# Pooled attention with a squared-relu feed-forward: the front written in another order, plain copies of probabilities, relu first in a step, longer groups of idle products

## The chip, the core and the metric

The kernel runs on one core of a Trainium2 chip. It uses five engines, each with a queue of its own that is worked off in order: TensorE (PE, with its weight loads as PEld), VectorE (DVE), ScalarE (ACT), GpSimd (POOL), and SyncE (SP), which here only issues DMAs. The metric is the device time of one execution in microseconds, the median of three runs. Lower is better.

## The reference

Attention with eight heads over 8 batches of 576 tokens, in which keys and values are averaged over groups of 8 tokens (72 keys remain), and then a feed-forward layer whose activation is the square of a relu. All is float32.

```python
k_p = k.reshape(B, H, Sp, pool, D).mean(axis=3)      # 576 keys -> 72
v_p = v.reshape(B, H, Sp, pool, D).mean(axis=3)
scores = scale * np.matmul(q, k_p.transpose(0, 1, 3, 2))
scores = scores - np.max(scores, axis=-1, keepdims=True)
attn = np.exp(scores)
attn = attn / (np.sum(attn, axis=-1, keepdims=True) + 1e-09)
x = np.matmul(attn, v_p)             # then heads side by side: [4608, 512]
h = np.maximum(x @ w_in, 0.0)        # w_in [512, 2048]
out = h * h @ w_out                  # w_out [2048, 512]
```

## The kernel before

The 4608 tokens are worked in 12 chunks of 384 (`CH`). A chunk's feed-forward is 16 steps (`NFC`), one for each block of 128 hidden columns: `hidden` forms the block's products with `w_in` (tile `h`), `activate` applies relu and square on ScalarE (tile `r`), and two steps later (`LAG`) `project` multiplies by `w_out` and adds into three accumulators (tile `o`). The attention of a later chunk is spread over the steps of the chunks ahead of it by the table `work`, which holds for each step the functions to run in it. In chunk 0 the first six blocks use plain float32 products (8 records per `h`); from then on operands are split into a high part (made by ScalarE) and a low part (made by VectorE), with three products of each pair.

Ahead of step 0 stands the front, written out by hand: the attention of chunk 0, when nothing is there to hide it. Names in traces: `k`, `q`, `v`, `vv` are loads; `kp` pooled keys, each in two copies; `kps`, `qps` transposes of keys and queries on TensorE, which ScalarE copies to `kf` and `st`; `sps` the scores of one pair of heads; `tm` their maxima and `te` their exponentials (`token_scores`); `token_normalise` divides `te` by its sums on VectorE; `pps` are `te` turned by TensorE (`token_turn`) and copied to `sc` by ScalarE; `vps` pooled values (`pool_v_pair`); `av` the weighted values (`weigh_values`), copied to `x`. There are four pairs of heads. `idle` are products of the identity whose result nobody reads (`keep_busy(n)`: n products, two records each). Chunk 1 runs the same token-wise functions inside chunk 0's steps (table `EARLY`); later chunks use another form.

The weights arrive as float32 words in `raw_i` (from `w_in`) and `raw_o` (from `w_out`), 512 KB each, and pass through `magnitude` (two instructions on ScalarE) and, a step later, `to_float32` (three on VectorE per tile; two tiles as a rule), giving `wf_i` and `wf_o`; `split_weights` then makes `w_i`, `w_o`. So in chunk 0 ScalarE and VectorE prepare weights while TensorE already uses them. `split_x0` makes `xh` and `xl` from chunk 0's `x`.

Within a step the instructions are written in this order: `hidden`; the attention's products; `project`; what follows on those products; the other work of the step (`magnitude` among it); `to_float32`; `split_weights`; the DMA issues; `activate`. Each engine keeps that order. All instructions carry line 34, that of the recording helper, in the profile.

Of the kernel before, what the change touches and what calls it, by code (L numbers as in the profile page):

```python
# [37 lines left out]
def pooled_attn_relu2_ffn(  # L38
# [35 lines left out]
    SCALE = 1.0 / (D ** 0.5) / POOL  # L74
    LAG, QL = 2, 4

    IDLE = (10, 2)
    STB, SCB, LD, OB = 1, 2, 4, 3


# [5 lines left out]

    STEADY = ((-22, -18, -14, -10), (0, 1, 3, 4, 5, 6, 7, 8))
    KV0 = -35
    EARLY = ((-16, -13, -10, -7), (0, 1, 2, 3, 4))

    KV_AT = ((0, 1, 4, 5, 8, 9), (2, 3, 6, 7, 10, 11), (7, 12), (12, 13, 16, 17, 20, 21, 24, 25))
    NKT = H * SP_ // QT
# [121 lines left out]
    def pool_k(b, i):  # L214
        if i % KT == 0:
            loaded["kp", b, i // KT] = sb.tile([QT, KT, 2, D], F32, name=f"kp_{b}_{i}", tag="kp", bufs=2)
        kp, kt = loaded["kp", b, i // KT][:, i % KT], loaded.pop(("k", b, i))
        if b == 1:
            by_halves(kp[:, 0, :], kt)
            GP.tensor_tensor(kp[:, 1, :], kt[:, :D], kt[:, D:2 * D], op=ALU.add)  # L220
        else:
            DVE.tensor_reduce(kp[:, 0, :], kt.rearrange("p (o d) -> p d o", d=D), axis=AX.X, op=ALU.add)
            DVE.tensor_copy(kp[:, 1, :], kp[:, 0, :])

    def new_batch(b):
        if b not in kv:
# [171 lines left out]

    def token_banks(c, p, name, tag):
        if c:
            return [ps_a.tile([P, 512], F32, name=f"{name}_{c}_{p}_{j}", tag="a") for j in range(2)]
        if tag == "h":
            return [ps_h.tile([P, 512], F32, name=f"{name}_{c}_{p}_{j}", tag="h") for j in range(2)]
        return [ps_o.tile([P, 512], F32, name=f"{name}_{c}_{p}_{j}", tag=f"o{(2 * p + j) % NTT}") for j in range(2)]

    def token_scores(c, p):
        st = live.pop((c, p))
        ss = token_banks(c, p, "sps", "o")  # L410
        segs = segments(c)
        for t in range(NQ):
            h, b = 2 * p + t // 2, segs[t % 2 % len(segs)][0]
            for j in range(2):
                two = slice(j * D, (j + 1) * D)
                PE.matmul(ss[j][:QT, t * SP_:(t + 1) * SP_], lhsT=st[two, t * QT:(t + 1) * QT],
                          rhs=kf[b][two, h // KH, h % KH * SP_:(h % KH + 1) * SP_], start=True, stop=True)
        views = [x[:QT, :NQ * SP_].rearrange("p (t n) -> p t n", t=NQ) for x in ss]

        def then():  # L420
            m = sb.tile([QT, 4, 2, NQ], F32, name=f"tm_{c}_{p}", tag="tm", bufs=2)
            e = w_tile(F32, f"te_{c}_{p}")[:QT, :, :NQ * SP_].rearrange("p i (t n) -> p i t n", t=NQ)
            e = [e[:, i] for i in range(2)]
# [12 lines left out]

        return then
# [10 lines left out]
    def token_turn(c, p):  # L448
        e, _ = live.pop((c, p))
        pt = token_banks(c, p, "pps", "h")  # L450
        for i in range(2):
            for t in range(NQ):
                PE.transpose(pt[i][:SP_, t * QT:(t + 1) * QT], e[t // 2][:, i * 2 + t % 2], ident[:QT, :QT])

        def then():
            sc = sb.tile([SP_, 2, CH], F32, name=f"sc_{c}_{p}", tag="sc", bufs=SCB)
            order = "p (s t two) -> p two t s" if len(segments(c)) == 1 else "p (t s two) -> p two t s"
# [9 lines left out]
    def split_x0():  # L467
        xts[0] = [sb.tile([P, NPAIR, CH], F32R, name=f"{x}_0", tag=x, bufs=2) for x in ("xh", "xl")]
        for i, x in enumerate(x0):
            split(*(t[:, 2 * i:2 * i + 2] for t in xts[0]), x)  # L470

    def weigh_values(c, p):

# [7 lines left out]
        for b, o, n in segments(c):  # L481
            for i in range(2):
                PE.matmul(av[i * D:(i + 1) * D, o:o + n], lhsT=kv[b][2][:, 2 * p + i, :], rhs=sc[:, i, o:o + n],
                                 start=True, stop=True)

        def then():
            if c == 0:
# [51 lines left out]
    def project(c, fc):  # L539
# [12 lines left out]
        def store():  # L552
            for t in range(NTT):
                ob = sb.tile([P, DM], F32, name=f"ob_{c}_{t}", tag="ob", bufs=OB)
                ACT.copy(ob, accs[c][t])
                dma(out[c * CH + t * P:c * CH + (t + 1) * P, :], ob)

        return store if fc == NFC - 1 else None

# [4 lines left out]
    def at(step, f, *a):  # L564
        work.setdefault(max(step, -PRO), []).append((f, a))
# [26 lines left out]
        land(key)  # L592
    issue_loads()
    keep_busy(IDLE[0])
    for i in range(KT + 2):
        pool_k(0, i)
    transpose_k(0, 0)()
    transpose_q(0, 0)()
    transpose_q(0, 1)()
    pool_k(0, KT + 2)  # L600
    keep_busy(IDLE[1])
    after = [token_scores(0, 0), transpose_k(0, 1)]
    for f in after:
        f()
    after = [pool_v_pair(0, 0), pool_v_pair(0, 1), token_scores(0, 1)]
    for f in reversed(after):
        f()
    after = [pool_v_pair(0, 2), pool_v_pair(0, 3)]
    transpose_q(0, 2)()
    transpose_q(0, 3)()  # L610
    for f in after:
        f()
    for i in range(NKT):
        pool_k(1, i)
    new_batch(1)
    for h in range(H):
        pool_v(1, h)
    for p in range(NPAIR):
        token_normalise(0, p)
        after = [token_scores(0, p + 2)] if p + 2 < NPAIR else []  # L620
# [63 lines left out]
    for s in range(-PRO, len(steps) + LAG):  # L684
# [51 lines left out]
```

## Time and profile before

| | |
|---|---|
| median of 3 runs | 964.59 us (963.69 to 967.23) |
| the profiled execution | 964.33 us |
| its span, first to last instruction | 962.6 us |
| TensorE busy | 946.1 us, 98% |
| VectorE busy | 615.0 us, 64% |
| ScalarE busy | 451.5 us, 47% |
| GpSimd busy | 348.8 us, 36% |

Shares are means over a long steady part and a short first one. The front and the steps of chunk 0 fill about the first eighth of the span, and it is there that TensorE has gaps and a lower clock. A start in a timeline is the time at which an instruction began; where several run one after the other, the distance of two starts is what one of them costs its queue, and the duration that is shown holds a tail that overlaps with the next.

### The profile page before, as it was taken

How to read it: one execution, taken by the hardware profiler on the slowest of the kernel's cores; microseconds unless marked ns; L12 is line 12 of the kernel's file. 1: busy time of each engine (PE TensorE's matmuls, PEld its weight loads, DVE VectorE, ACT ScalarE, POOL GpSimd, SP SyncE). 2: the span in 40 equal slices, each digit the busy share in tenths (PEclk: the TensorE clock that was granted, in tenths of full speed). 3: DMA queues.
4: the chain of work that ended last, by engine and by line, in shares of the span. 5: the costliest groups of instructions: out<-in, count | busy, mean ns of one | idle time of the engine just before them, and what ended most of it. 6: DMA issues, size and time to landing. Idle time of an engine off the chain costs nothing.

```text
span 962.6 us, 13481 instructions
## 1 busy us (share of the span) xinstructions
PE 946.1 (98%) x4944; PEld 803.6 (83%) x4944; DVE 615.0 (64%) x1028; ACT 451.5 (47%) x909; POOL 348.8 (36%) x215
## 2 busy tenths in 40 slices
PE   7899999999999999999999999999999999999998
PEld 6456668888888888888888888888888888888997
DVE  7889886667865566677765656767776565453221
ACT  3789776754444344444344344434443434532322
POOL 3800144444444434344353444344443534440000
PEclk9799999999999999999999999999999999999999
DMA  9963112113112112112112112112211110100000
GB/s 256 319 237 116 61 33 78 35 50 98 52 31 77 32 34 67 48 52 82 52 44 77 30 35 79 38 30 69 82 50 39 68 32 18 58 10 9 33 1 34
DMA packets 51651, 63.65 MB, mean 66 GB/s; under 512 B 13936, under 2 KB 32192, under 8 KB 51584
## 3 DMA queue, kind: packets, MB, share of 16 engines
q1 hardware_dynamic: 51584, 62.78, 21.2%
q8 instruction: 39, 0.64, 0.3%
q14 instruction: 28, 0.23, 0.1%
HBM read 53.08 MB, written 9.68 MB: 65 GB/s over the span
## 4 chain that ended last, share of the span: by engine, by line
PE 88%; DVE 5%; DMA 4%; ACT 2%; issue 1%; SPq 0%; ACTq 0%; DVEq 0%
PE o L34 41%; PE h L34 39%; PE av L34 3%; PE sps L34 3%; DVE wf_o L34 2%; DVE wf_i L34 1%; PE qps L34 1%; DMA raw_o<-in_moe_w_out_dram 1%; DMA v<-in_v_dram 1%; DMA k<-in_k_dram 1%; ACT te L34 1%; DMA vv<-in_v_dram 1%; DMA raw_i<-in_moe_w_in_dram 1%; DVE tm L34 1%; DVE w_i L34 1%
## 5 line engine op out<-in xcount | busy, mean ns | idle before, releaser
L34 PE MATMUL h<-xh,w_i 128*128 128x384 f32 x1488 | 416.9, 341 | 0.0
L34 PE MATMUL o<-w_o,gh 128*128 128x512 f32 x1056 | 334.8, 398 | 0.0
L34 PEld LDWEIGHTS h<-xh,w_i 128*128 128x128 f32 x1488 | 272.8, 188 | 10.6 <-issue 1.4
L34 POOL PARTITION_ALL_REDUCE tot<-sc x80 | 201.4, 2564 | 210.1 <-issue 199.6
L34 PE MATMUL h<-xl,w_i 128*128 128x384 f32 x744 | 249.9, 336 | 0.0
L34 PEld LDWEIGHTS o<-w_o,gh 128*128 128x128 f32 x1056 | 192.4, 188 | 51.9 <-issue 16.5
L34 POOL PARTITION_ALL_REDUCE mx<-sc x80 | 117.8, 1519 | 287.1 <-ACT sc L34 287.1
L34 DVE TENSOR_TENSOR gl<-r,gh 128x384 fp32r<-128x384 f32 x176 | 143.5, 815 | 109.1 <-ACT gh L34 108.9
L34 PE MATMUL o<-w_o,gl 128*128 128x512 f32 x528 | 209.1, 396 | 0.0
L34 DVE TENSOR_TENSOR r<-r 128x384 f32<-128x384 f32 x160 | 105.6, 660 | 109.1 <-ACT r L34 108.8
L34 ACT CAST gh<-r 128x384 fp32r<-128x384 f32 x176 | 90.4, 514 | 150.3 <-DVE r L34 149.8
L34 PEld LDWEIGHTS h<-xl,w_i 128*128 128x128 f32 x744 | 139.7, 188 | 10.6 <-issue 2.9
L34 ACT ACTIVATE r<-h 128x384 f32<-128x384 f32 x192 | 94.2, 491 | 100.5 <-PE h L34 99.1
L34 PEld LDWEIGHTS o<-w_o,gl 128*128 128x128 f32 x528 | 99.1, 188 | 22.1
L34 DVE TENSOR_TENSOR st<-qps,st 64x384 fp32r<-64x384 f32 x80 | 60.8, 760 | 59.1 <-ACT st L34 58.3
L34 ACT CAST st<-qps 64x384 fp32r<-64x384 f32 x80 | 59.5, 744 | 56.9 <-PE qps L34 56.5
L34 ACT CAST xh<-rb 128x384 fp32r<-128x384 f32 x40 | 20.5, 513 | 94.6 <-DVE rb L34 94.6
L34 ACT ACTIVATE sc<-sc 72x384 f32<-72x384 f32 x80 | 39.7, 525 | 46.4 <-DVE sc L34 46.4
L34 DVE TENSOR_REDUCE vp<-v 72x64 f32<-72x512 f32 x48 | 51.0, 1062 | 0.0
L34 PE MATMUL av<-sc,vp 72*64 72x384 f32 (+1 forms) x256 | 45.6, 436 | 3.6 <-ACT sc L34 2.1
L34 PE MATMUL o<-wf_o,r 128*128 128x512 f32 x96 | 44.4, 598 | 0.0
L34 DVE TENSOR_REDUCE kp<-k 96x64 f32<-96x512 f32 x42 | 43.8, 1043 | 0.2 <-DMA k<-in_k_dram 0.2
(82 smaller groups left out, 702.1 us busy)
## 6 DMA issues: line engine op xcount, KB each, us to landing
k<-in_k_dram SPq DMA_DIRECT2D x48, 192.0 KB
out_dram<-ob SPq DMA_DIRECT2D x36, 256.0 KB
raw_i<-in_moe_w_in_dram SPq DMA_DIRECT2D x16, 512.0 KB
raw_o<-in_moe_w_out_dram SPq DMA_DIRECT2D x16, 512.0 KB
v<-in_v_dram SPq DMA_DIRECT2D x56, 144.0 KB
rb<-rd SPq DMA_DIRECT2D x80, 96.0 KB
q<-in_q_dram SPq DMA_DIRECT2D x30, 192.0 KB
q<-in_q_dram SPq DMA_DIRECT2D x32, 96.0 KB
```

The costliest lines, as they stand in the source:

```text
L34: return lambda *a, **k: self.tc.keep_in_program_order(f(*a, **k))
```

## The change

It has six parts.

1. The front is written in another order. Pooled keys and scores of the first two pairs come first; the pooling of values moves from one place behind the first scores into the loop over the pairs, ahead of each `token_turn`. The second copy of batch 0's pooled keys moves from VectorE to ScalarE.
2. The front's softmax takes the form that chunk 1 had already: instead of a VectorE subtraction and two ScalarE exponentials of 288 columns, two small VectorE multiplications and eight ScalarE exponentials of 72 columns with a bias.
3. `token_turn` copies probabilities to `sc` as they stand instead of into token order. The columns of chunks 0 and 1 thus stay in another order down to `out`, where the store puts the rows back: six stores of 32 to 96 rows for a chunk instead of three of 128. Chunk 1's `weigh_values` reads its columns in two strided groups.
4. In chunk 0's steps `activate` is written ahead of the step's other work instead of last.
5. Groups of idle products have six products instead of two, and there are nine of them after the first group of ten instead of five.
6. `split_x0` is done in two halves in steps 3 and 4 instead of in one in step 3, and chunk 1's first pair starts one step later.

```diff
-    IDLE = (10, 2)
+    IDLE = (10, 6)
-    EARLY = ((-16, -13, -10, -7), (0, 1, 2, 3, 4))
+    EARLY = ((-15, -13, -10, -7), (0, 1, 2, 3, 4))
...
-            DVE.tensor_copy(kp[:, 1, :], kp[:, 0, :])
+            (DVE.tensor_copy if b else ACT.copy)(kp[:, 1, :], kp[:, 0, :])
...
             for i in range(2):
                 DVE.tensor_reduce(m[:, 0, i], views[i], axis=AX.X, op=ALU.max)
-                if c:
-                    DVE.tensor_scalar(m[:, 1, i], m[:, 0, i], -SCALE, None, op0=ALU.mult)
-                else:
-                    DVE.tensor_tensor(e[i], views[i], m[:, 0, i].unsqueeze(2).to_broadcast([QT, NQ, SP_]), op=ALU.subtract)
+                DVE.tensor_scalar(m[:, 1, i], m[:, 0, i], -SCALE, None, op0=ALU.mult)
             for i in range(2):
-                if c == 0:
-                    ACT.activation(e[i], e[i], AF.Exp, scale=SCALE)
-                for t in range(NQ if c else 0):
+                for t in range(NQ):
                     ACT.activation(e[i][:, t], views[i][:, t], AF.Exp, bias=m[:, 1, i, t:t + 1], scale=SCALE)
...
-                ACT.copy(sc[:, i].rearrange(order, t=NQ // 2, two=2),
-                         pt[i][:SP_, :CH].rearrange("p (two t s) -> p two t s", t=NQ // 2, two=2))
+                ACT.copy(sc[:, i], pt[i][:SP_, :CH])
...
+                rows = rows.rearrange("(s t two) d -> two t s d" if c == 0 else "(t s two) d -> two t s d", t=2, two=2)
+                for n in range(NQ):
+                    lo, hi = max(n * QT, t * P), min((n + 1) * QT, (t + 1) * P)
+                    if lo < hi:
+                        dma(rows[n // 2, n % 2, lo - n * QT:hi - n * QT, :], ob[lo - t * P:hi - t * P, :])
...
     for p in range(NPAIR):
-        token_normalise(0, p)
-        after = [token_scores(0, p + 2)] if p + 2 < NPAIR else []
+        f = pool_v_pair(0, p)
+        if p + 2 < NPAIR:
+            g = token_scores(0, p + 2)
+            f()
+            token_normalise(0, p)
+            g()
+        else:
+            f()
+            token_normalise(0, p)
         if p:
+            keep_busy(IDLE[1])
             weigh_values(0, p - 1)()
-        keep_busy(IDLE[1])
+            keep_busy(IDLE[1])
         if p == 2:
             for key in first_keys:
                 magnitude(key)
         token_turn(0, p)()
-        for f in after:
-            f()
     to_float32(*first_keys)
+    keep_busy(IDLE[1])
     weigh_values(0, NPAIR - 1)()
...
-    at(3, split_x0)
+    for i in range(2):
+        at(3 + i, split_x0, i)
...
         for f in later:
             f()
+        if activate and s < NFC:
+            activate()
+            activate = None
         for f, a in todo:
```

Three places show how the queues change. First TensorE's queue in the second half of the front, from the idle products behind `av` of pair 1 to `av` of pair 3. Before:

```order
L34 MATMUL idle_0_444<-ident 128x128 x2
L34 MATMUL pps_2_0_452<-ident,te_2_381 72x96 x4
L34 MATMUL pps_2_1_453<-ident,te_2_381 72x96 x4
L34 MATMUL av_2_471<-sc_2_462,vp_184 64x384 x2
L34 MATMUL idle_0_475<-ident 128x128 x2
L34 MATMUL pps_3_0_478<-ident,te_3_427 72x96 x4
L34 MATMUL pps_3_1_479<-ident,te_3_427 72x96 x4
L34 MATMUL av_3_497<-sc_3_488,vp_184 64x384 x2
```

And after the change:

```order
L34 MATMUL idle_0_486<-ident 128x128 x6
L34 MATMUL pps_2_0_498<-ident,te_2_364 72x96 x4
L34 MATMUL pps_2_1_499<-ident,te_2_364 72x96 x4
L34 MATMUL vps_3_511<-vv_3_101,ones 72x128 x6
L34 MATMUL idle_0_525<-ident 128x128 x6
L34 MATMUL av_2_532<-sc_2_508,vp_179 64x384 x2
L34 MATMUL idle_0_536<-ident 128x128 x6
L34 MATMUL pps_3_0_543<-ident,te_3_415 72x96 x4
L34 MATMUL pps_3_1_544<-ident,te_3_415 72x96 x4
L34 MATMUL idle_0_562<-ident 128x128 x6
L34 MATMUL av_3_569<-sc_3_553,vp_179 64x384 x2
```

The groups of idle products are three times as long, one more stands ahead of each `av`, and the pooled values `vps` of the pair stand in the queue too.

Next ScalarE's queue in steps 2 and 3 of chunk 0 (two weight tiles' `magnitude` and the relu and square `r_2`), up to the first cast of `x` to `xh`. Before:

```order
L34 ACTIVATE wf_i_0_604<-raw_i_2_519 128x512
L34 ACTIVATE raw_i_2_519<-raw_i_2_519 128x512
L34 ACTIVATE wf_o_633<-raw_o_520 128x512
L34 ACTIVATE raw_o_520<-raw_o_520 128x512
L34 ACTIVATE r_2_655<-h_2_620 128x384
L34 ACTIVATE r_2_655<-r_2_655 128x384
L34 COPY sc_0_681<-pps_0_0_663 72x2x192
L34 COPY sc_0_681<-pps_0_1_664 72x2x192
L34 COPY st_0_553<-qps_1_673 128x384
L34 CAST xh_685<-x_0_404 128x768
L34 CAST xh_685<-x_1_405 128x768
```

And after the change:

```order
L34 ACTIVATE r_2_703<-h_2_668 128x384
L34 ACTIVATE r_2_703<-r_2_703 128x384
L34 ACTIVATE wf_i_0_655<-raw_i_2_591 128x512
L34 ACTIVATE raw_i_2_591<-raw_i_2_591 128x512
L34 ACTIVATE wf_o_708<-raw_o_592 128x512
L34 ACTIVATE raw_o_592<-raw_o_592 128x512
L34 COPY st_0_648<-qps_1_729 128x384
L34 ACTIVATE r_3_738<-h_3_724 128x384
L34 ACTIVATE r_3_738<-r_3_738 128x384
L34 CAST xh_741<-x_0_435 128x768
```

`r_2` and `r_3` now stand ahead of the magnitudes of their steps and `r_3` ahead of `xh`; of `xh` only the first half stands here.

Last VectorE's queue at the normalising of chunk 1's first pair (`tm_0`, `te_0`) and the low part `xl` of chunk 0's `x`. Before:

```order
L34 TENSOR_REDUCE tm_0_588<-te_0_589 96x4 x2
L34 TENSOR_SCALAR tm_0_588<-tm_0_588 96x8
L34 RECIPROCAL tm_0_588<-tm_0_588 96x8
L34 TENSOR_TENSOR te_0_589<-te_0_589,tm_0_588 96x288 x2
L34 TENSOR_SCALAR wf_o_516<-wf_o_516 128x512
L34 TENSOR_SCALAR wf_i_0_604<-wf_i_0_604 128x512
L34 SCALAR_TENSOR_TENSOR wf_o_516<-wf_o_516,raw_o_119 128x512
L34 SCALAR_TENSOR_TENSOR wf_i_0_604<-wf_i_0_604,raw_i_0_509 128x512
L34 SCALAR_TENSOR_TENSOR wf_o_516<-raw_o_119,wf_o_516 128x512
L34 SCALAR_TENSOR_TENSOR wf_i_0_604<-raw_i_0_509,wf_i_0_604 128x512
L34 TENSOR_TENSOR xl_686<-x_0_404,xh_685 128x768
L34 TENSOR_TENSOR xl_686<-x_1_405,xh_685 128x768
```

And after the change:

```order
L34 SCALAR_TENSOR_TENSOR wf_o_588<-raw_o_119,wf_o_588 128x512
L34 SCALAR_TENSOR_TENSOR wf_i_0_655<-raw_i_0_581,wf_i_0_655 128x512
L34 TENSOR_TENSOR xl_742<-x_0_435,xh_741 128x768
L34 TENSOR_REDUCE tm_0_689<-te_0_690 96x4 x2
L34 TENSOR_SCALAR tm_0_689<-tm_0_689 96x8
L34 RECIPROCAL tm_0_689<-tm_0_689 96x8
L34 TENSOR_TENSOR te_0_690<-te_0_690,tm_0_689 96x288 x2
```

The normalising stood ahead of the tiles `o119` and `i509` and of both `xl`; now it stands behind the same two tiles (the second is named `i581`) and behind the first `xl`.

## Rows read from the trace of the kernel before

**Rows 1.** Windows of the span: busy per engine, granted clock, DMA share.
```profile
26.00:33.00 7.00, 4.52 (x27) 2.32 (x26) 6.62 (x17) 6.00 (x12) 6.07 (x12) 0.99 0.90 254
...
33.00:43.00 10.00, 9.65 (x25) 4.85 (x24) 5.90 (x10) 5.37 (x10) 9.37 (x13) 0.50 1.03 389
...
100.00:120.00 20.00, 17.69 (x89) 11.93 (x88) 15.89 (x31) 13.69 (x31) 3.38 (x2) 1.00 0.11 37
...
160.00:960.00 800.00, 799.14 (x4179) 701.75 (x4177) 484.63 (x768) 338.59 (x670) 298.76 (x150) 1.00 0.15 47
```

**Rows 2.** TensorE's timeline in the front: start, us, what, [idle before].
```profile
8.29 0.84 PE L34 MATMUL qps<-ident,k 96*128 96x96 f32 x4
...
12.08 2.81 PE L34 MATMUL vps<-vv,ones 96*72 96x128 f32 x24 [0.49 <-DMA vv<-in_v_dram]
...
21.96 0.71 PE L34 MATMUL idle<-ident 128*128 128x128 f32 x4
...
22.29 0.39 PE L34 MATMUL idle<-ident 128*128 128x128 f32 x2
...
22.51 0.83 PE L34 MATMUL pps<-ident,te 96*72 96x96 f32 x8
...
23.27 0.90 PE L34 MATMUL sps<-kf,st 64*96 64x72 f32 x16
...
24.10 1.42 PE L34 MATMUL av<-sc,vp 72*64 72x384 f32 x4
...
39.83 4.47 PE L34 MATMUL h<-x,wf_i 128*128 128x384 f32 x8
```

**Rows 3.** TensorE's timeline in chunk 0's steps.
```profile
49.73 2.85 PE L34 MATMUL h<-x,wf_i 128*128 128x384 f32 x8 [1.17 <-ACT r L34]
...
56.20 2.85 PE L34 MATMUL h<-x,wf_i 128*128 128x384 f32 x8 [1.04 <-ACT r L34]
...
58.88 0.82 PE L34 MATMUL pps<-ident,te 96*72 96x96 f32 x8
...
59.88 2.77 PE L34 MATMUL o<-wf_o,r 128*128 128x512 f32 x6
...
102.29 0.87 PE L34 MATMUL av<-sc,vp 72*64 72x192 f32 x8 [1.56 <-ACT te L34]
```

**Rows 4.** ScalarE's timeline.
```profile
23.05 1.56 ACT L34 COPY sc<-pps 72x384 f32<-72x384 f32 x2 [1.00 <-PE pps L34]
...
40.31 0.67 ACT L34 ACTIVATE wf_o<-raw_o 128x512 f32<-128x512 f32 x1
...
45.96 0.69 ACT L34 COPY kf<-kps 128x288 f32<-128x288 f32 x2
...
51.72 1.78 ACT L34 ACTIVATE te<-sps,tm 96x72 f32<-96x72 f32 x8 [1.48 <-DVE tm L34]
...
55.62 0.53 ACT L34 ACTIVATE r<-h 128x384 f32<-128x384 f32 x1
...
60.97 1.58 ACT L34 CAST xh<-x 128x768 fp32r<-128x768 f32 x2
```

**Rows 5.** VectorE's timeline.
```profile
55.18 0.80 DVE L34 TENSOR_REDUCE tm<-te 96x4 f32<-96x288 f32 x2
...
57.19 0.42 DVE L34 TENSOR_SCALAR wf_o<-wf_o 128x512 f32<-128x512 f32 x1
...
61.85 1.83 DVE L34 TENSOR_TENSOR xl<-x,xh 128x768 fp32r<-128x768 f32 x2 [1.50 <-ACT xh L34]
...
63.59 0.42 DVE L34 TENSOR_SCALAR wf_i<-wf_i 128x512 f32<-128x512 f32 x1
...
66.67 0.70 DVE L34 TENSOR_TENSOR w_i<-wf_i,w_i 128x512 fp32r<-128x512 f32 x1
...
67.27 0.46 DVE L34 TENSOR_REDUCE tm<-sps 96x4 f32<-96x288 f32 x1
```

**Rows 6.** SyncE's issues of the stores: ns min/median/max.
```profile
L34 SPq DMA_DIRECT2D out_dram<-ob x36: 332/362/1040, 145.2 to 959.8; - x36
```

More of the change, by code (lines that the diff above doesn't have):

```diff
@@ L456, in then @@
             sc = sb.tile([SP_, 2, CH], F32, name=f"sc_{c}_{p}", tag="sc", bufs=SCB)
-            order = "p (s t two) -> p two t s" if len(segments(c)) == 1 else "p (t s two) -> p two t s"
             for i in range(2):
-                ACT.copy(sc[:, i].rearrange(order, t=NQ // 2, two=2),
-                         pt[i][:SP_, :CH].rearrange("p (two t s) -> p two t s", t=NQ // 2, two=2))
+                ACT.copy(sc[:, i], pt[i][:SP_, :CH])
             live[c, p] = (sc, None)
@@ L465, in pooled_attn_relu2_ffn, with split_x0 @@
     x0 = []
[L467 to L470, printed above, removed]
+    def split_x0(i):
+        if i == 0:
+            xts[0] = [sb.tile([P, NPAIR, CH], F32R, name=f"{x}_0", tag=x, bufs=2) for x in ("xh", "xl")]
+        split(*(t[:, 2 * i:2 * i + 2] for t in xts[0]), x0[i])
     def weigh_values(c, p):
@@ L480, in weigh_values @@
         av = ps_a.tile([P, 512], F32, name=f"av_{c}_{p}", tag="a")
-        for b, o, n in segments(c):
+        segs = segments(c)
+        for t, (b, o, n) in enumerate(segs):
             for i in range(2):
-                PE.matmul(av[i * D:(i + 1) * D, o:o + n], lhsT=kv[b][2][:, 2 * p + i, :], rhs=sc[:, i, o:o + n],
-                                 start=True, stop=True)
+                x, y = av[i * D:(i + 1) * D, :CH], sc[:, i]
+                if c == 1:
+                    x, y = (a.rearrange("p (two t s) -> p t two s", two=2, t=2)[:, t] for a in (x, y))
+                elif c:
+                    x, y = x[:, o:o + n], y[:, o:o + n]
+                PE.matmul(x, lhsT=kv[b][2][:, 2 * p + i, :], rhs=y, start=True, stop=True)
         def then():
@@ L555, in store @@
                 ACT.copy(ob, accs[c][t])
-                dma(out[c * CH + t * P:c * CH + (t + 1) * P, :], ob)
+                rows = out[c * CH:(c + 1) * CH]
+                if c > 1:
+                    dma(rows[t * P:(t + 1) * P, :], ob)
+                    continue
+                rows = rows.rearrange("(s t two) d -> two t s d" if c == 0 else "(t s two) d -> two t s d", t=2, two=2)
[3 more added lines that the diff above has]
+                        dma(rows[n // 2, n % 2, lo - n * QT:hi - n * QT, :], ob[lo - t * P:hi - t * P, :])
         return store if fc == NFC - 1 else None
@@ L594, in pooled_attn_relu2_ffn @@
     keep_busy(IDLE[0])
-    for i in range(KT + 2):
+    for i in range(KT):
         pool_k(0, i)
@@ L598, in pooled_attn_relu2_ffn @@
     transpose_q(0, 0)()
+    keep_busy(IDLE[1])
+    pool_k(0, KT)
+    f = token_scores(0, 0)
     transpose_q(0, 1)()
+    f()
+    pool_k(0, KT + 1)
+    keep_busy(IDLE[1])
+    f = token_scores(0, 1)
     pool_k(0, KT + 2)
-    keep_busy(IDLE[1])
-    after = [token_scores(0, 0), transpose_k(0, 1)]
-    for f in after:
-        f()
[L605 to L608, printed above, removed]
     transpose_q(0, 2)()
+    f()
+    transpose_k(0, 1)()
     transpose_q(0, 3)()
-    for f in after:
-        f()
     for i in range(NKT):
@@ L618, in pooled_attn_relu2_ffn @@
     for p in range(NPAIR):
-        token_normalise(0, p)
-        after = [token_scores(0, p + 2)] if p + 2 < NPAIR else []
+        f = pool_v_pair(0, p)
+        if p + 2 < NPAIR:
+            g = token_scores(0, p + 2)
+            f()
+            token_normalise(0, p)
+            g()
+        else:
+            f()
+            token_normalise(0, p)
         if p:
+            keep_busy(IDLE[1])
             weigh_values(0, p - 1)()
-        keep_busy(IDLE[1])
+            keep_busy(IDLE[1])
         if p == 2:
@@ L627, in pooled_attn_relu2_ffn @@
         token_turn(0, p)()
-        for f in after:
-            f()
     to_float32(*first_keys)
+    keep_busy(IDLE[1])
     weigh_values(0, NPAIR - 1)()
```

## Prediction

> **What bounds the kernel now.** I read the windows of the span first, to see where TensorE is not the bound. From 160 to 960 us it is busy 799.14 of 800 us at the full clock; the change touches nothing there except the order of the columns of chunk 1 and the stores of two chunks, so what it is worth is decided in the first 120 us [rows 1]. There, from 26 to 33 TensorE is busy 4.52 of 7 us; from 33 to 43 the granted clock is 0.50, the lower of the two levels (1.2 GHz); and from 100 to 120 it is busy 17.69 of 20 at the full clock, so 2.3 us are lost [rows 1]. Then I read TensorE's own timeline for the price of each kind of product and for what ended its waits [rows 2, 3], and last those of ScalarE and VectorE, which make what TensorE waits for [rows 4, 5]. The first `h` starts at 39.83 and takes 4.47 us at the low clock; a like one takes 2.85 at the full clock [rows 2, 3]. In the steps the third and fourth `h` wait 1.17 and 1.04 us for ScalarE's `r`, and an `av` waits 1.56 at 102 us [rows 3].
>
> **The front.** TensorE now has 54 idle products in groups behind the first ten instead of 10. Two idle products (four records) start at 21.96, their last two records at 22.29, and the next work at 22.51: 0.55 us for a group of two, 0.11 for each further record, so a group of six (eight records more) costs 0.55 + 0.88 = 1.43 [rows 2]. Nine of them are 12.9 us, five of the old 2.75: 10.2 us of work are added. Before, this stretch was full of waits, so most of it is hidden; what counts is whether the queue without any wait is longer than before. Its pieces are, by distances of starts or durations less their tails: `vps` four times 1.37 (12.08, two pairs in 2.81) 5.5; `pps` four times 0.76, 3.0; `sps` four times 0.83, 3.3; `av` four times some 1.37, 5.5; four more groups of transposes at about 0.35, 1.4 [rows 2]. From the first transposes, over by about 8.9 (8.29 plus half a microsecond), that is 8.9 + 12.9 + 5.5 + 3.0 + 3.3 + 5.5 + 1.4 = 40.5. I add 1.1 for two waits for ScalarE's copies that no idle group covers (the second half's pooled keys, and `kf` of that half; two such copies take 0.57 [rows 4]; 0 and 2 are the ends). The first `h` then starts at about 41.6: **+1.8**. The ends are +0.7 without the two waits and +3 with longer ones.
>
> The softmax of one pair of heads is 1.06 us of maxima (67.27, two reduces and two small multiplications), 1.65 of exponentials (51.72 less its tail) and 2.01 of normalising (from 55.18 to 57.19): 4.7 us [rows 4, 5]. One pair's share of TensorE's queue with two idle groups, `vps`, `pps`, `sps` and `av` is 7.2 us, so the new form of the softmax, and ScalarE's copies of pooled keys under the first idle products, cost nothing; without that cover a late normalising would cost up to 2.0 each. The plain copies to `sc` save ScalarE perhaps a third of the 1.56 that two took [rows 4]; TensorE's queue is the bound there, so I put that at nothing too.
>
> **The clock.** The fall at 33 follows a stretch in which TensorE was busy two thirds of the time, and the change fills that stretch with products [rows 1]. I expect the full clock up to the first `h` and behind it: 4.47 becomes 2.85, **-1.6** [rows 2, 3]. The Trainium skill (TensorE: Matmul & The Clock Gate, "What's actually happening") says that the throttled level is the default and that activity releases it; the fall behind the sparse stretch agrees, and by it the -1.6 comes. Its Part 4 there, "PE-mode transpose", says that transposes don't count as activity in the same way; no run here shows that yet, and by it the first rival below would come.
>
> **Relu first.** ScalarE gets to the last front copy some 2.0 us later than before (at 41.95; the magnitudes behind it stood at 40.31 and now follow at 42.3). Then come five pairs of magnitudes (from 40.31 to 45.96 before, 5.65) to 48.0, `kf` 0.57, `r_0` 1.0, so the third `h` still waits about as long [rows 4]. But `r_1` now stands ahead of the fourth step's magnitudes: the 1.04 of the fourth `h` goes, less what ScalarE is late, **-0.8** [rows 3]. Against it, in step 1 the copy of chunk 1's queries `st` now comes behind another pair of magnitudes, at 52.2, while TensorE is at `sps_0` at 51.7: **+0.5**.
>
> **VectorE behind `xh`.** This is the largest term. The low part `xl` needs ScalarE's `xh`, and stands now ahead of the normalising of chunk 1's first pair; before it stood behind it (rows of the order above). Before, VectorE waited 1.50 there [rows 5]. ScalarE after `r_0` (49.6): two pairs of magnitudes at 1.13, 51.9; `st` 0.4; `r_1` 1.0, 53.2; two pairs, 55.5; `te_0` 1.65, 57.1; `r_2` 1.0; two pairs, 60.4; `st` 0.4; `r_3` 1.0; so `xh`'s first half starts at 61.7 and, at half of 1.58, is there at 62.5 [rows 4]. VectorE has its maxima by 56.0 and one pair of tiles (from 63.59 to 66.67, 3.08) by 59.1, and then waits some 3.5 us: `xl` half of 1.83 to 63.4, normalising 2.01 to 65.4 [rows 5]. TensorE reaches `pps_0` at 64.1 (two `h` at 2.7 and two `o` at 2.6 behind `sps_0` [rows 3]); its first product needs only the first half of `te`: **+1.0**. What stands behind it in TensorE's queue is `sps_1` and the whole feed-forward. Before, `pps_0` at 58.88 had no wait [rows 3].
>
> The same again a step later: VectorE does a pair and a split (0.60) to 69.1, `tm_1` to 70.2, and waits 3.0 us for the second `xh` (ScalarE: `te_1` from 69.7, `r_4`, `xh` at 72.4); then `xl`, a pair and the split of the first `w_i` end at 77.7 [rows 4, 5]. TensorE stands at `h_6`, the first block that needs split weights, at 75.3 and at the product that needs the low part of them at 76.5: **+1.2**. The next normalising (2.01) ends at 80.2, when TensorE has reached `pps_1` at 78.9: **+1.3**. From there two pairs are some 2 us behind their places, and the `av` that waited 1.56 waits about **1.1 more**. Each of these four lies between 0 (ScalarE and VectorE catch up in the stretch's idle time) and about twice the value.
>
> **At nothing.** The stores: SyncE issues one in 0.36 us (median of 36), so six more are 2.2 us of a queue that has 800 us; uncovered, behind the last of a chunk, about 1 us [rows 6]. The strided reads in chunk 1's `weigh_values` are bounded by the `av` of 0.87 for eight records, four of them: between 0 and 1 us in all [rows 3]; I take 0.
>
> **The sum.** 1.8 - 1.6 - 0.8 + 0.5 + 1.0 + 1.2 + 1.3 + 1.1 = +4.5. The profiled execution took 964.33, 0.26 below the median of the runs, so 968.8.
>
> **Rivals.** (a) The clock falls in the front all the same, as it did at 33 with half-filled queues: then ten microseconds at 0.50 do the work of five, and the queue, which has no slack now, ends 5.1 later: 973.9, slower. For it: idle products and transposes are what fills the queue. Against it: from 26 to 33, with such groups in it, the clock was still 0.99 [rows 1]. It decides from about 2 us at half clock on (1 us lost). (b) VectorE's lateness is absorbed: the four terms behind `xh` and that of `st` (5.1) vanish, and 1.8 - 1.6 - 0.8 = -0.6 gives 963.7. For it: VectorE waits for ScalarE there, and each does less than it could; against it, both waits lie in a chain of `te`, `r` and `xh` that is written in that order. (c) The other sign: on top of (b) the two waits of the front do not occur (-1.1) and the freed ScalarE takes away the third `h`'s 1.17 and the 2.3 lost from 100 to 120: 963.7 - 1.1 - 1.2 - 2.3 = 959.1, faster; it decides where at least 4.6 of these 5.2 us come. Against it: the rows at 100 us wait for chunk 1's softmax, on which only its place has changed [rows 3].
>
> **Chances.** The forecast, 966.5 to 971: 0.50. (b), 962.5 to 966.5: 0.25. (c), below 962.5: 0.12. (a), above 971: 0.13. The range 961.5 to 971.5 leaves out (a) and half of (c), 0.19; the likeliest case alone is 966.5 to 971. A difference of 0.5% (4.8 us) is about what a measurement of this kernel can tell from no change: below 959.8 lies half of (c), 0.06; above 969.4 all of (a) and 0.21 of the forecast, 0.34; between them 0.60.
>
> **What the profile would show.** A granted clock of 1.00 from 9 us on, the first `h` at 41.6 and 2.85 long; no wait for `r` at the fourth `h`; VectorE waiting over 3 us for `xh` twice; waits of 1 us or more at `pps_0`, `h_6` and `pps_1`. The prediction is wrong if VectorE meets no such wait, if the front's queue still has many waits (then it is longer than 40.5), or if the clock falls.

## The result and the profile after

The changed kernel took 966.94 us (median of 20 runs, 965.63 to 969.64) beside 964.39 for the kernel before (20 runs on the same chip); the ratio is 1.0023, 95% interval 1.0012 to 1.0033: slower by 2.2 us (1.2 to 3.2). The two medians alone lie 2.6 us apart, the means of the same runs 2.2. The forecast was 968.8 with a range of 961.5 to 971.5, and 0.60 on a change of less than 0.5%; that came in. The profiled execution took 966.62 with a span of 964.9, 2.3 above the span of before.

The windows of the changed kernel (columns as in [rows 1]):

```profile
9.00:26.00 17.00, 16.51 (x175) 14.44 (x175) 14.37 (x36) 11.26 (x47) 9.35 (x21) 1.00 1.06 294
26.00:33.00 7.00, 7.00 (x63) 6.28 (x62) 4.51 (x11) 4.03 (x10) 6.53 (x12) 1.00 0.90 259
33.00:43.00 10.00, 10.00 (x64) 7.09 (x64) 5.18 (x7) 5.33 (x11) 9.22 (x16) 1.00 1.04 392
60.00:80.00 20.00, 16.56 (x82) 9.61 (x81) 16.21 (x37) 15.43 (x36) 0.00 (x0) 1.00 0.33 105
100.00:120.00 20.00, 17.22 (x90) 11.50 (x90) 16.75 (x33) 14.32 (x34) 3.33 (x2) 1.00 0.15 55
```

One of these windows in the kernel before, which [rows 1] does not have:

```profile
60.00:80.00 20.00, 20.00 (x90) 11.65 (x88) 16.62 (x35) 18.16 (x41) 0.00 (x0) 1.00 0.45 142
```

In the profiled execution the granted clock is 1.00 from 9 us to the end of these windows, where before it was 0.50 from 33 to 43 [rows 1]. In the front TensorE waits only once, 0.43 us at 16.66 for `kf`. But it loses 3.4 us between 60 and 80 us, where before it was busy all the time, and 2.8 instead of 2.3 between 100 and 120. Its timeline, first the front, then the steps:

```profile
16.66 0.90 PE L34 MATMUL sps<-kf,st 64*96 64x72 f32 x16 [0.43 <-ACT kf L34]
...
22.41 0.87 PE L34 MATMUL av<-sc,vp 72*64 72x384 f32 x4
23.21 1.60 PE L34 MATMUL idle<-ident 128*128 128x128 f32 x12
...
38.86 2.85 PE L34 MATMUL h<-x,wf_i 128*128 128x384 f32 x8
...
46.24 2.84 PE L34 MATMUL h<-x,wf_i 128*128 128x384 f32 x8 [1.10 <-ACT r L34]
49.44 0.90 PE L34 MATMUL sps<-kf,st 64*96 64x72 f32 x16 [0.36 <-ACT st L34]
...
52.95 2.74 PE L34 MATMUL h<-x,wf_i 128*128 128x384 f32 x8
...
63.18 1.06 PE L34 MATMUL pps<-ident,te 96*72 96x96 f32 x8 [1.98 <-DVE te L34]
...
75.99 0.62 PE L34 MATMUL h<-xh,w_i 128*128 128x384 f32 x2 [0.30 <-DVE w_i L34]
...
78.10 1.06 PE L34 MATMUL pps<-ident,te 96*72 96x96 f32 x8 [1.14 <-DVE te L34]
...
104.43 0.87 PE L34 MATMUL av<-sc,vp 72*64 72x192 f32 x8 [2.08 <-ACT te L34]
```

The first `h` starts at 38.86 and takes 2.85 us (before 39.83 and 4.47 [rows 2]). By the fourth `h` TensorE is 3.25 us ahead of before (52.95; before 56.20, where it waited for `r` [rows 3]). Then come waits that before had not: 1.98 us at `pps_0`, 0.30 within the seventh `h`, 1.14 at `pps_1`; and the `av` that waited 1.56 [rows 3] waits 2.08 and starts 2.14 later than before. The new waits are 3.94 us together, 0.7 more than the lead; the other 1.4 lie in groups that run longer without a wait that the profile lists (`pps_0` 0.99 us to the next start, before 0.67; the `sps` behind it 1.13, before 0.83). From the `av` to the end the distance hardly grows: 2.3 at the end. VectorE's timeline shows what TensorE waits for:

```profile
52.78 0.44 DVE L34 TENSOR_REDUCE tm<-sps 96x4 f32<-96x288 f32 x1
...
60.53 0.96 DVE L34 TENSOR_TENSOR xl<-x,xh 128x768 fp32r<-128x768 f32 x1 [3.48 <-ACT xh L34]
61.40 0.80 DVE L34 TENSOR_REDUCE tm<-te 96x4 f32<-96x288 f32 x2
...
71.30 0.96 DVE L34 TENSOR_TENSOR xl<-x,xh 128x768 fp32r<-128x768 f32 x1 [2.99 <-ACT xh L34]
...
102.70 0.44 DVE L34 TENSOR_REDUCE tm<-sps 96x4 f32<-96x288 f32 x1
```

VectorE waits 3.48 and 2.99 us for `xh` (before 1.50 [rows 5]); the normalising of chunk 1's first pair begins only behind the first of these waits, at 61.40 (before 55.18 [rows 5]). The first row is the maximum of chunk 1's first pair, the last row that of its last pair; `te` of the last pair is what the `av` at 104.43 waits for. The last row in the kernel before:

```profile
100.55 0.46 DVE L34 TENSOR_REDUCE tm<-sps 96x4 f32<-96x288 f32 x1
```

So VectorE comes to this place 2.15 us later, TensorE to the `av` 2.14 and the kernel to its end 2.3 later.

### The profile page after: what moved, and what is told of

The parts are those of the page before. It is cut to its first block, busy times and chain, and to the rows that moved or that the text cites. A ratio compares the mean times of both kernels' runs of the same rounds, so it can differ in the third digit from the quotient of the medians.

```text
span 964.9 us, 13692 instructions
## 1 busy us (share of the span) xinstructions
PE 949.7 (98%) x5032; PEld 810.9 (84%) x5032; DVE 612.6 (63%) x1022; ACT 453.2 (47%) x939; POOL 346.7 (36%) x215
## 4 chain that ended last, share of the span: by engine, by line
PE 88%; DVE 5%; DMA 4%; ACT 2%; issue 1%; SPq 0%; DVEq 0%; ACTq 0%
PE o L34 41%; PE h L34 39%; PE av L34 3%; PE sps L34 3%; DVE wf_i L34 2%; DVE wf_o L34 1%; PE qps L34 1%; DMA raw_o<-in_moe_w_out_dram 1%; DMA v<-in_v_dram 1%; DMA k<-in_k_dram 1%; DVE tm L34 1%; ACT te L34 1%; DMA vv<-in_v_dram 1%; DMA raw_i<-in_moe_w_in_dram 1%; DVE w_i L34 1%
## 5 line engine op out<-in xcount | busy, mean ns | idle before, releaser
L34 PE MATMUL av<-sc,vp 72*64 72x384 f32 (+1 forms) x256 | 41.6, 425 | 2.1 <-ACT te L34 2.1
```

The lines of the kernel that those rows point to most:

```text
L34: return lambda *a, **k: self.tc.keep_in_program_order(f(*a, **k))
```

## The experiments

Theory A, after the first look: the front and relu first gain, and the sixth part loses, by VectorE's waits for `xh` ahead of the normalising. Its rivals: B, the longer idle groups cost the time; C, relu first does. All ratios are to the kernel before on the same chip; its medians there were 964.1 to 964.6. Where two of the kernels are set beside each other, the difference is that of their medians; by their ratios it comes out up to 1 us otherwise.

**Low part behind the normalising.** `split_x0` keeps ScalarE's copy; VectorE's subtraction becomes a function of its own, written behind the other work of the step.

```diff
-        split(*(t[:, 2 * i:2 * i + 2] for t in xts[0]), x0[i])
+        ACT.copy(xts[0][0][:, 2 * i:2 * i + 2], x0[i])
+    def low_x0(i):
+        hi, lo = (t[:, 2 * i:2 * i + 2] for t in xts[0])
+        DVE.tensor_tensor(lo, x0[i], hi.bitcast(F32), op=ALU.subtract)
...
             for d, f in zip(offsets, names):
                 at(s + d, f, c, p)
+    for i in range(2):
+        at(3 + i, low_x0, i)
```

> The changed kernel with one difference: in steps 3 and 4 the low part of x0 (VectorE) is written behind the normalising of chunk 1's pair, while the high part (ScalarE) stays in its place. Theory A (the time is lost where VectorE waits for xh ahead of the normalising): the wait of 1.98 us at pps_0 goes, VectorE's wait in front of xl falls from 3.48 to about 1.5, later waits stay; about 965.0, 2.0 below the changed kernel, ratio to the kernel before 1.000. Theory B (the longer groups of idle products cost the time): no change, 967, ratio 1.0023. Theory C (relu first makes ScalarE late): no change either.

965.12 us, ratio 1.0009 (0.9998 to 1.0020). The expected wait at `pps_0` is gone; part of it comes back as a wait of the scores behind it. TensorE's timeline of this kernel:

```profile
61.24 0.83 PE L34 MATMUL pps<-ident,te 96*72 96x96 f32 x8
...
63.99 0.90 PE L34 MATMUL sps<-kf,st 64*96 64x72 f32 x14 [1.60 <-ACT sc L34]
```

VectorE's timeline of it:

```profile
60.80 0.96 DVE L34 TENSOR_TENSOR xl<-x,xh 128x768 fp32r<-128x768 f32 x1 [1.48 <-ACT xh L34]
...
100.97 0.45 DVE L34 TENSOR_REDUCE tm<-sps 96x4 f32<-96x288 f32 x1
```

The scores of the second pair need a bank that `pps_0` leaves only when ScalarE has copied it to `sc`. VectorE waits 1.48 there instead of 3.48 and is at the last maximum 1.7 us earlier than in the changed kernel; the median is 1.8 lower, though the intervals of the two ratios overlap. This is theory A's place and size.

**Both high parts in step 3.** In addition:

```diff
-        at(3 + i, split_x0, i)
+        at(3, split_x0, i)
```

> As the first of these kernels, and both high parts of x0 are made in step 3, so that the second low part in step 4 finds its high part done. Theory A: VectorE's second wait for xh (2.99 us) goes too, and with it the waits of TensorE for w_i (0.30) and pps_1 (1.14): about 963.5, ratio 0.999. Theories B and C: 967, ratio 1.0023.

964.94 us, ratio 1.0004 (0.9990 to 1.0018). VectorE's second wait for `xh` and TensorE's at `pps_1` are gone, as expected, but the time hardly moved against the first kernel and stayed 1.4 us above theory A's 963.5: the scores wait 1.75 us for `sc`, and VectorE is at the last maximum at 100.80, where the first kernel has 100.97.

**Groups of two idle products in the changed kernel.**

```diff
-    IDLE = (10, 6)
+    IDLE = (10, 2)
```

> The changed kernel with groups of two idle products instead of six (nine groups, and the first of ten as before). Theory B: 36 products fewer are 7.9 us less in TensorE's queue, and the time falls by 3 us or more, to 964 or below. Theory A: the waits that the products filled come back, the granted clock falls to 0.50 near 33 us again and the first h takes 4.4 us; the time stays within 1.5 us of 967.

964.51 us, ratio 1.0007 (0.9998 to 1.0016), 2.4 less than the changed kernel (the intervals of the two ratios overlap): between the two expectations. Its TensorE timeline:

```profile
32.56 2.85 PE L34 MATMUL h<-x,wf_i 128*128 128x384 f32 x8
...
60.56 1.55 PE L34 MATMUL pps<-ident,te 96*72 96x96 f32 x8 [4.61 <-DVE te L34]
```

VectorE's, at the maximum of chunk 1's first pair:

```profile
50.16 0.44 DVE L34 TENSOR_REDUCE tm<-sps 96x4 f32<-96x288 f32 x1
```

Windows of it (columns as in [rows 1]):

```profile
33.00:43.00 10.00, 8.40 (x34) 5.01 (x32) 9.11 (x12) 9.97 (x21) 9.21 (x15) 1.00 1.04 391
60.00:80.00 20.00, 19.44 (x86) 12.05 (x87) 16.80 (x38) 15.48 (x36) 0.00 (x0) 0.85 0.46 147
```

The front ends 6.3 us earlier, and the fall near 33 that theory A expected did not come in this execution: TensorE was busy 6.81 of 7 us from 26 to 33 (before 4.52), and the clock was 1.00. But VectorE, already busy 9.11 of 10 us from 33 to 43 (5.18 in the changed kernel), is only 2.6 us earlier at chunk 1's first maximum (50.16 for 52.78), and it keeps that distance to the last one, at 100.09. At `pps_0` TensorE waits 4.61 us for it, and the clock falls in that wait (0.85 from 60 to 80). Of 6.3 us, 2.4 are left.

**Relu last in the changed kernel** (the block that writes `activate` ahead of the step's other work is taken out).

> The changed kernel with activate written last in chunk 0's steps, as before. Theory C: time falls by 1 us or more, to 966 or below. Theory A: the fourth h waits for r again (some 1 us), while xh starts one relu and square (1 us) earlier and VectorE's wait in front of xl shrinks by that: within 1 us of 967, ratio 1.0015 to 1.003.

966.45 us, ratio 1.0022 (1.0012 to 1.0032): not to be told from the changed kernel, as theory A expected. Beside the sixth part, relu first is worth nothing either way.

**The sixth part undone.**

```diff
-    EARLY = ((-15, -13, -10, -7), (0, 1, 2, 3, 4))
+    EARLY = ((-16, -13, -10, -7), (0, 1, 2, 3, 4))
...
-        at(3 + i, split_x0, i)
+        at(3, split_x0, i)
```

> The changed kernel with its sixth part undone: both halves of x0 are split in step 3 and chunk 1's first pair starts one step earlier, as before; front, idle groups and relu first stay. Theory A (the sixth part is what loses the time, by VectorE's waits for xh ahead of the normalising and by pps_0 and the scores of the second pair in one step): the 3.3 us that TensorE has gained by the fourth h of the changed kernel stay, no wait of over 1 us at pps_0 or h_6: about 961.5, ratio 0.997. Theory B (idle products): 967, ratio 1.0023.

966.09 us, ratio 1.0018 (1.0009 to 1.0026). Theory A fails here as it was put: the waits at `pps_0` are gone (0.26), VectorE is as early as before, and yet the time fell by only 0.9 instead of 5. TensorE's timeline (of an execution of 964.85, 1.2 below the median):

```profile
52.46 2.85 PE L34 MATMUL h<-x,wf_i 128*128 128x384 f32 x8 [0.28 <-ACT r L34]
...
73.34 0.45 PE L34 MATMUL h<-xh,w_i 128*128 128x384 f32 x1 [0.69 <-ACT w_i L34]
...
102.10 0.89 PE L34 MATMUL av<-sc,vp 72*64 72x192 f32 x8 [2.14 <-ACT te L34]
```

VectorE's:

```profile
100.36 0.45 DVE L34 TENSOR_REDUCE tm<-sps 96x4 f32<-96x288 f32 x1
```

And the window behind the `av`:

```profile
102.80:106.20 3.40, 3.40 (x8) 1.50 (x5) 1.70 (x2) 3.33 (x8) 0.00 (x0) 0.50 0.00 0
```

TensorE is 3.7 us ahead of before at the fourth `h`, gives it up in waits (0.69 for `w_i`, 0.68 at `pps_1`, 2.14 at the `av`), and arrives at the `av` at 102.10, 0.2 before the kernel before: it can't get past VectorE. Behind this last wait the granted clock is 0.50 from 102.8 to 106.2. The mean granted clock is on record for each of the eleven executions: the profiled one and three others have 0.998 or more and took 963.5 to 964.9; the other seven, with 0.995 or 0.996, lost more by the clock, at places that are not on record, and took 965.9 to 967.5.

**The three later pairs of chunk 1 one step later**, on top of the kernel with both high parts in step 3:

```diff
-    EARLY = ((-15, -13, -10, -7), (0, 1, 2, 3, 4))
+    EARLY = ((-15, -12, -9, -6), (0, 1, 2, 3, 4))
```

> As the kernel with both high parts of x0 in step 3 and the low part behind the normalising, and the three later pairs of chunk 1 each one step later, so that the scores of the second pair no longer stand in the step in which the first pair is turned. Theory A: the wait of 1.75 us of these scores for ScalarE's copies goes: about 963.2, ratio 0.9985. If instead chunk 1's end, one step later, comes too late for its first h, the time rises to 966 or more.

966.24 us, ratio 1.0021 (1.0011 to 1.0032): the wait of the scores is gone, but the last pair comes too late, and TensorE waits 3.80 us for its `te` at 108.85.

**The kernel before with groups of six.**

```diff
-    IDLE = (10, 2)
+    IDLE = (10, 6)
```

> The kernel before with one difference: groups of six idle products instead of two (five groups). Theory A: the clock stays full, the first h takes 2.85 instead of 4.47 us and the av at half clock shorten, against 4.4 us of products of which the waits of that front hide the most: between 962.5 and 965, ratio 0.998 to 1.0005. Theory B: four microseconds slower, ratio 1.004.

966.44 us, ratio 1.0020 (1.0010 to 1.0030). Slower by 2.3, half of what B expected and 1.4 above the 965 that A allowed. In the old front the idle products do lengthen the queue (the first `h` starts at 42.32, at the full clock), and `av` still waits for `sc` up to 1.38 us.

**The kernel before with relu first.**

> The kernel before with one difference: relu first in chunk 0's steps. Theory A: the fourth h loses its wait of 1.04 us for r, and little is given back: about 963.7, ratio 0.999. Theory C (relu first makes xh, te and the copies late): slower, ratio above 1.0005.

968.22 us, ratio 1.0045 (1.0032 to 1.0059): theory C's sign, and the largest cost of any one part. TensorE's timeline:

```profile
37.44 2.85 PE L34 MATMUL h<-x,wf_i 128*128 128x384 f32 x8
...
52.30 2.85 PE L34 MATMUL h<-x,wf_i 128*128 128x384 f32 x8 [1.33 <-ACT r L34]
...
73.23 0.44 PE L34 MATMUL h<-xh,w_i 128*128 128x384 f32 x1 [0.71 <-ACT w_i L34]
...
103.19 1.54 PE L34 MATMUL av<-sc,vp 72*64 72x192 f32 x8 [1.75 <-ACT te L34]
```

VectorE's:

```profile
84.14 0.46 DVE L34 TENSOR_REDUCE tm<-sps 96x4 f32<-96x288 f32 x1 [0.85 <-PE sps L34]
```

Windows of the same execution:

```profile
26.00:33.00 7.00, 4.53 (x25) 2.21 (x24) 6.64 (x16) 6.18 (x11) 6.37 (x13) 1.00 0.94 276
33.00:43.00 10.00, 9.34 (x44) 5.39 (x44) 8.47 (x13) 7.55 (x14) 9.45 (x12) 1.00 1.05 381
103.20:109.90 6.70, 6.70 (x15) 2.95 (x15) 4.29 (x8) 5.68 (x13) 0.00 (x0) 0.50 0.06 21
```

Two things are to be seen. The front is that of the kernel before, and its queues are as sparse (4.53 of 7 us busy from 26 to 33), but in this execution the clock did not fall at 33: the first `h` starts at 37.44 and takes 2.85. So this front can run without the fall of [rows 1]; how often it does is seen further down. And TensorE, 3.9 us ahead of before at the fourth `h`, is 0.9 behind it at the `av`: behind the waits at 73 and 75 us (0.71 and 0.67) the clock is 0.50 from 76 to 79, VectorE then waits 0.85 for the late scores, its last maximum is at 101.46, and behind the wait of the `av` the clock is 0.50 once more.

**The front alone** (parts 1, 2, 3 and 5; the kernel with the sixth part undone, and relu last as well).

> The kernel before with the changed front, plain copies and longer idle groups, and its old steps (relu last, both halves of x0 in step 3, chunk 1's first pair at its old place). Theory D (the front alone costs time: without the fall of the clock at 33 us, which the kernel before with relu first did not show with the same front, the old front ends at 37.4 and the new one at 38.9): 965.5 to 966.3, ratio 1.001 to 1.002. Theory A (the front gains 1 us and only the steps lose): 963.6 or less, ratio 0.999 or less.

963.49 us, ratio 0.9981 (0.9962 to 0.9999): faster than the kernel before, as A expected, against theory D, though the interval ends close to 1. Set beside the kernel with the sixth part undone it differs by relu last alone, and is 2.6 us faster; set beside the changed kernel with relu last it differs by the sixth part alone, and is 3.0 faster; in both the intervals lie apart. Its TensorE timeline:

```profile
48.44 5.49 PE L34 MATMUL h<-x,wf_i 128*128 128x384 f32 x8 [1.74 <-ACT r L34]
...
102.39 0.87 PE L34 MATMUL av<-sc,vp 72*64 72x192 f32 x8 [1.30 <-ACT te L34]
```

VectorE's:

```profile
100.64 0.45 DVE L34 TENSOR_REDUCE tm<-sps 96x4 f32<-96x288 f32 x1
```

In the profiled execution (964.59, the slowest of its twelve) the clock fell at the third `h` (5.49 us); nothing of that is left at 102 us, where this kernel and the kernel before stand within 0.1 us. At an equal mean clock the front alone shows no gain: its six executions with 0.998 took 962.2 to 964.0, three of the kernel before with 0.998 took 962.4 to 962.8. Its gain goes with a clock that falls less: 0.996 or more in all twelve, where the kernel before mostly has 0.991 to 0.995.

**Groups of two and the low parts behind the normalising** (the second and the third kernel above in one).

> The changed kernel with groups of two idle products, both high parts of x0 in step 3, and the low parts behind the normalising. If both savings (2.0 and 2.4) add up: 962.5, ratio 0.998. Theory E (ScalarE and VectorE, which wait for each other in the steps, have the split weights of the seventh h ready at about 73 us whatever the front does, since that h began between 73.2 and 74.4, or waited until then, in seven of the nine kernels that were traced): 964.2, ratio 1.000, with more waits ahead of that h and the seventh h again at about 73.

963.55 us, ratio 0.9976 (0.9953 to 1.0000): between the two expectations, which it does not decide. The seventh `h` begins at 72.77, and ScalarE waits 4.28 us at 49.06 for a buffer that GpSimd's last pooling of values frees.

**Splits first, groups of two, sixth part undone.**

```diff
         if activate and s < NFC:
             activate()
             activate = None
+        for f, a in todo:
+            if f is split_weights:
+                f(*a)
         for f, a in todo:
             if f not in on_pe + last:
                 f(*a)
...
-        for f, a in todo:
-            if f is split_weights:
-                f(*a)
```

> The changed kernel with groups of two idle products, its sixth part undone (both halves of x0 in step 3, chunk 1's first pair at its old place), and in each step split_weights written ahead of the magnitudes and of to_float32. Theory E: the split weights are there some 2 us earlier, the seventh h begins by 71.5 and the time falls to about 962, ratio 0.9975. If the seventh h still waits until 73, theory E names the wrong link, and the time is 964 or more.

972.45 us, ratio 1.0071 (1.0050 to 1.0092), and the seventh `h` begins at 73.59. By the expectation theory E names the wrong link; but this `h` starts without a wait, directly behind the `o` before it, so the run does not test the theory: TensorE came late for another reason. ScalarE's timeline:

```profile
50.46 1.77 ACT L34 ACTIVATE te<-sps,tm 96x72 f32<-96x72 f32 x8 [7.76 <-POOL vp L34]
52.10 0.51 ACT L34 ACTIVATE r<-h 128x384 f32<-128x384 f32 x1
```

TensorE's:

```profile
52.67 5.49 PE L34 MATMUL h<-x,wf_i 128*128 128x384 f32 x8 [6.89 <-ACT r L34]
```

Chunk 1's first `te` waits 7.76 us for GpSimd's last `vp`, which ends at 50.4 (by the code, `te` takes its buffer from the ring that also holds the values this `vp` is made from). Since `r_1` stands behind that `te`, the fourth `h` waits 6.89, and the clock falls (5.49 for that `h`). In the front alone and with the sixth part undone the last `vp` is over by 44.5 us, and `te` starts at 50.05 and 50.25, behind VectorE's maxima (from 49.25 and 49.45). Here the maxima come from 45.66 on, 4 us earlier, and `te` starts at 50.46 all the same.

**Idle products ahead of the waiting `av`**, on the kernel with the sixth part undone:

```diff
+        if (c, p) == (1, 2):
+            t = ps_h.tile([P, 512], F32, name="idle_h", tag="h")
+            for _ in range(8):
+                PE.matmul(t[:, :P], lhsT=ident, rhs=ident, start=True, stop=True)
         av = ps_a.tile([P, 512], F32, name=f"av_{c}_{p}", tag="a")
```

> The kernel with the changed front and relu first, but the old split of x0 and the old place of chunk 1's first pair (966.1 when it was timed), and eight idle products more in TensorE's queue just ahead of the av that waits 2.1 us at 102 us in it. In that kernel's profile the granted clock is 0.50 behind this wait, where the kernel with relu last shows 1.00, and relu first cost 2.6 us. Theory F (what relu first costs is that fall of the clock behind a longer wait): the wait shrinks to some 0.3 us, the clock stays full behind it, and the time falls to about 963.5, ratio 0.998 to 0.9995. If the fall is not what relu first costs: 966, ratio 1.0015 to 1.002.

965.02 us, ratio 1.0000 (0.9988 to 1.0013), 1.1 less than without them (the intervals overlap a little), and between the two expectations. TensorE's timeline:

```profile
99.77 1.98 PE L34 MATMUL idle_h<-ident 128*128 128x128 f32 x16
102.05 0.87 PE L34 MATMUL av<-sc,vp 72*64 72x192 f32 x8 [0.30 <-ACT te L34]
```

A window of it:

```profile
100.00:120.00 20.00, 18.95 (x96) 13.24 (x96) 15.64 (x30) 13.55 (x31) 3.37 (x2) 1.00 0.11 36
```

The wait is 0.30, the clock stays at 1.00, and 1.1 us come back: the fall is part of what relu first costs, but not the whole of its 2.6. The front alone measured 1.5 less still, and what makes that difference stays open: the profiled executions of the two (spans 962.5 and 962.8) don't show it.

## Where the time is set

A table of the profiled executions: the start of VectorE's maximum of chunk 1's last pair (as in the rows above), the span, and the granted clock from 100 to 120 us.

| kernel | last maximum | span | difference | clock 100 to 120 |
|---|---|---|---|---|
| before | 100.55 | 962.6 | 862.1 | 1.00 |
| changed | 102.70 | 964.9 | 862.2 | 1.00 |
| both high parts early | 100.80 | 963.0 | 862.2 | 1.00 |
| groups of two | 100.09 | 961.9 | 861.8 | 1.00 |
| front only | 100.64 | 962.8 | 862.2 | 1.00 |
| groups of two, low behind | 99.25 | 961.0 | 861.8 | 1.00 |
| idle ahead of `av` | 100.32 | 962.5 | 862.2 | 1.00 |
| low behind | 100.97 | 963.8 | 862.8 | 0.91 |
| relu last | 101.71 | 964.5 | 862.8 | 0.91 |
| sixth part undone | 100.36 | 963.1 | 862.7 | 0.91 |
| before, groups of six | 101.80 | 964.5 | 862.7 | 0.91 |
| before, relu first | 101.46 | 965.7 | 864.2 | 0.83 |
| splits first | 105.68 | 971.8 | 866.1 | 0.83 |

Each row is one execution. In all of these kernels TensorE waits at the `av` behind this maximum, 1.3 to 2.5 us (0.30 behind the idle products). Where the clock stays full behind it, the end stands 861.8 to 862.2 us behind this one instruction of VectorE, whatever TensorE did before: 6.3 us of shorter front or 3.4 of longer steps. A fall of the clock ahead of it (front only, groups of two) leaves no trace in the difference; one behind it adds 0.6 or, with 0.83, 2 and more. (In the kernel with the later pairs this instruction stands a step later, and it is left out.)

## Why the prediction came out as it did

The time lies in the range, and the sign of the sum was right; its size, 4.5 for 2.2, was not. The front was mis-sized, and adding it to the steps was wrong too: with groups of two the front is 6.3 us shorter and the end only 2.4 earlier.

**The front: wrong, +1.8 forecast, -1.0 measured.** The term that fails is the price of "`av` four times some 1.37, 5.5". The row of 1.42 [rows 2] held a wait inside its group, for the second copy to `sc`. The groups of `sc` in the kernel before, with who waited for it (us, times), show it:

```profile
L34 PE MATMUL av<-sc,vp x4: 486/512/537, 24.1 to 25.0; 72*64 72x384 f32 x4
L34 ACT COPY sc<-pps x3: 842/856/925, 23.0 to 26.6; 72x384 f32<-72x384 f32 x3
...
  PE av L34: 0.6, 1
```

The same groups in the changed kernel:

```profile
L34 ACT COPY sc<-pps x4: 474/487/517, 20.7 to 25.6; 72x384 f32<-72x384 f32 x4
...
L34 PE MATMUL av<-sc,vp x4: 486/512/537, 22.4 to 22.8; 72*64 72x384 f32 x4
```

The plain copies take 487 instead of 856 ns each, and an idle group stands behind them, so the products of the two heads now run at once: 0.80 us from one start to the next (22.41 to 23.21), not 1.37, which is 2.3 for four. The `av` of 0.87 for eight records of half the length [rows 3] had shown that price already. The two waits that were put at 1.1 measured 0.43. Together 3.0 of 41.6, so 38.6; the row has 38.86. The idle group itself was right: 1.43 forecast, 1.44 measured (23.21 to 24.65).

**The clock: right in the front, and in part taken back behind it.** 2.85 instead of 4.47 came. The same old front in the kernel before with relu first kept the full clock in its profiled execution; against that one the new front is 1.4 longer than the old one (38.86 to 37.44), against the profiled one of before 1.0 shorter. How often the old kernel's clock falls can be read from the mean granted clock of each execution, which does not say where a fall lay. Beside the experiments the kernel before was timed 105 times; without three that took 970 us or more, 78 of 102 have 0.991 to 0.995, like the profiled one (0.994), whose only fall is that at 33. Three have 0.998 and took 962.4 to 962.8, 1.6 to 1.9 below the medians of their chips: about the forecast's 1.6. (Of the rest, 17 have 0.984 and took about 967.5.) So a fall of this size is the rule and not the price of one execution, though its place is known for the profiled one alone. But the profile of the changed kernel, with 0.999, is not the rule there: five of its 20 executions have 0.998 or more and took 965.6 to 966.6, the other 15 have less, and their median is 967.4. At 0.998 or more the two kernels are thus some 3.3 us apart, in the median 2.6: by this estimate, from three and five executions, the change got 0.8 us from the clock and not 1.6. What the Trainium skill says of transposes (TensorE: Matmul & The Clock Gate, Part 4), no run here shows or refutes: the front of the changed kernel, made of transposes and other products, ran at 1.00.

**Relu first: the place right, the term wrong.** The fourth `h` has no wait, the third waits 1.10 as said, and `sps_0` waits 0.36 (0.5 forecast). But -0.8 is not what it is worth: alone on the kernel before it costs 4.1 us, on the new front 2.6, beside the sixth part 0.5 (not clear of noise), in part by the falls of the clock that follow its waits. From the first to the fourth `h` the changed kernel takes 14.1 us (38.86 to 52.95), the kernel before with groups of six and relu last 15.2 at the full clock (42.32 to 57.54): 1.1 are gained there, and waited off ahead of VectorE.

**VectorE behind `xh`: right.** 3.5 and 3.0 us of wait forecast, 3.48 and 2.99 measured; `pps_0` 1.98 (1.0: TensorE came 2.9 us earlier to it, the normalising only 2.0), `h_6` 0.30 (1.2), `pps_1` 1.14 (1.3), the `av` 0.52 more (1.1). Putting the low part behind the normalising alone gave back 1.8 us of the 2.2. The sum of 4.5 was too high by the front's 2.8, part of which came back as the longer wait at `pps_0`. That the 1.7 left of it is near the 2.2 measured is in part luck, since a lead of the front does not reach the end as it is.

**The rivals.** (a) did not occur in the profile, and the longest of the 20 executions, 969.64, is well below its 973.9. (b), the lateness absorbed, did not come: the waits did. (c), a faster kernel, did not come either, though the front alone measured less than before. What was absorbed is not VectorE's lateness but TensorE's lead. The price of each part depends on the others: with the new front, relu first alone costs 2.6, the sixth part alone 3.0, both 3.4.

## What to carry to other kernels

Where two engines bound a stretch alternately, price an edit at the place where the second one next holds up the first: here a lead of TensorE by 1 to 6 us in the front was worth 0 to 2.4 at the end, and 2 us of VectorE's queue were worth 2.2. A row that groups several instructions may hold a wait inside; take the price from one whose inputs were long there. Whether a stretch at the lower clock in one profile is the rule or the exception can be asked of the mean clock of the other executions, and a profile with a full clock needs the same question. Of the versions tried, the front without the new steps (0.9981) and the changed kernel with groups of two and the low part behind the normalising (0.9976) measured about 1 us less than the kernel before; for the second the interval reaches 1.0000, so that no gain is shown.

## What was not expected of the hardware

The products of two heads, each 64 columns of the array wide, run at the same time when both inputs are there: four records in 0.80 us, where with the second head's input 0.6 us late they took 1.35. A wait of 1.5 to 2.1 us at the `av` was followed by a clock of 0.50 in some executions and not in others (1.53, 1.75, 1.91, 2.09 and 2.14 us: yes; 1.56 once, 1.70 and 2.08 each in two kernels: no), so the length of the wait alone does not decide it; and one and the same front showed 0.50 at 33 us in one execution and 1.00 in another (of the kernel before with relu first).
